# Projecting the first group of heads with whole 128-row products, over the pieces of x as they come, in a two-branch attention kernel

## The chip, the cores and the metric

The kernel runs on one core of a Trainium2 chip. The metric is the device time of one execution in microseconds. The time before is 974.14 us, the median of 3 runs (971.82 to 974.33).

## The reference

Two attention branches read the same x (2048 tokens, 640 features; 32 heads of 20) and are mixed by a gate per token:

```python
g = _sigmoid((x * gate_w).sum(-1, keepdims=True))
a = _A_ref(x, A_wq, A_wk, A_wv, A_wo, A_beta)
b = _B_ref(x, B_wqkv, B_wo)
return g * a + (1 - g) * b
```

Branch A cuts the tokens into 4 segments of 512. Within a segment it computes causal softmax attention, and beside it reads a memory that the earlier segments have left (a 20 x 20 matrix and a vector per head, with phi(t) = t + 1 for positive t, exp(t) otherwise); `beta` mixes the two per head. Branch B is causal attention over a sliding window of 256 tokens. Each branch has its own output projection.

So the work is: the projections q, k and v of both branches (each a product with 640 input features, in 5 pieces of 128), the scores, exponentials and weighted sums, the memory, and two output projections. The result is in float32.

## The kernel before, in words

**Precision.** Every large product is made of three. An operand is split into a high part (rounded to fp32r, ScalarE, line 541) and a low part (the remainder, GpSimd or VectorE, line 558), and a product is high x high, high x low and low x high (`PAIRS`), summed in PSUM.

**Turns and units.** The 64 heads of both branches make 4 groups of 16. A turn T is one group in one segment (16 turns; T = 0 and T = 1 are the first group of each branch in the first segment). A turn has 4 units u of 4 heads each. For a turn, five row tiles `("m", T, 0..4)` of 128 x 512 hold q and k of the 16 heads, and four value tiles `("v", T, 0..3)` hold the values of 128 tokens each.

**Projection by halves.** `plan_qk` takes two row tiles at a time. Each product has only 64 of the 128 rows of the contraction (`gemm2`, line 604): half of the array works for the one tile, the other half for the other, side by side. A weight tile (128 x 640) holds rows 0 to 63 for one tile and 64 to 127 for the other. After all 5 pieces of x the second weight tile comes, in which the halves are exchanged, so that both tiles get the missing half of their rows. Between the two phases a `join` (an empty instruction on ScalarE or VectorE) makes the second half wait for the first. Values are done in the same way, two token blocks at a time (`v_mm`, line 753). The last output projection of the kernel uses whole 128-row products instead (`gemm`, line 596).

**After a row tile.** ScalarE and VectorE copy it from PSUM as high and low parts (`m_high`, 625; `m_low`, 629; a ring of two buffers), for the memory also as phi (666 to 674), and SP stores it to DRAM (`qk_store`, 654 to 661: two stores for tiles 0, 1, 3, 4, six for tile 2). A unit reads its stack of q and k back from there (`stack_read`, line 827, 1 MB for branch A).

**A unit.** 16 products give the scores for the row maxima (`max_mm`, 857), reduced on VectorE (867, with the readout 867); the maxima go through DRAM into spare rows of the stack (887, 891); then come the scores again, transposed (`st_mm`, 914), the exponentials on ScalarE (921), causal masks on GpSimd (927, 930), the sum with the values (`av_mm`, 946), and for branch A the memory's read and update (977, 997).

**Order of the work.** Each instruction is put into a plan with a due time t, in which one unit is 1.0. `Plan.order` simulates the engines, the DMA queues and the 8 PSUM banks, and picks at each moment, among the instructions that can start soonest, the one with the smallest due time; the picked order is the order of each engine's queue, which then runs strictly in it. `SHIFT` and `NUDGE` move due times by kind of instruction and by stretch of the plan. All loads and stores are issued by SP, in this one order.

**The start.** The weights go through 2 staging buffers (`NWS`) into a ring of 3 split tiles (`NW`). In the order of due times the first weight tile comes, then the 5 pieces of x, then the second and third weight tile. A weight tile's load waits for a free staging buffer, that is, for the split of the tile two before it; the split waits for the last product of the tile three before it. SP also fills padding rows in DRAM (line 509), loads the values' weights (575, 805 KB), and loads pieces of x for the next segment (line 550) as soon as buffers are free. 26 small products warm PE up before the first real one (line 444).

Of the kernel before, what the change touches and what calls it, by code (L numbers as in the profile page):

```python
# [57 lines left out]
KINDS = dict(v_mm="v", max_mm="x", st_mm="s", tiled_mm="t", mem_add="a", split_h="h", split_l="l", m_high="e", m_low="e", v_out="e",  # L58
# [30 lines left out]
    d={3: -1.3, 5: 1.3, 8: 1.2, 11: -0.1, 12: 1.3, 24: -0.6, 37: -2.7},
    e={22: -1.3, 28: 0.1, 33: -0.2, 38: -1.1, 40: 1.1, 47: -0.2, 52: 4.6, 59: 1.3},  # L90
    h={18: -0.9, 25: -2.3, 37: 1, 38: -1.9, 73: 2.2},
    k={40: 0.9},
    l={62: 1.3},
    m={2: -0.28, 24: 0.5, 28: 0.2, 32: -0.11, 34: -0.015, 38: 0.77, 39: 0.514, 41: 0.5, 42: -0.05, 43: -0.318, 44: 1,
       48: -0.04, 52: -0.26, 56: -0.13, 59: 0.027, 61: -0.06, 66: -0.137},
    p={16: -0.4, 32: 1.8, 33: 1.2, 42: 0.56},
    q={4: -0.011, 18: 0.7, 42: 2.1, 47: 0.6, 52: 0.2, 53: -1.2},
    r={11: 0.2, 14: -0.04, 18: -0.7, 19: 1.5, 31: 0.6, 34: 0.06, 40: 2.9, 49: 0.03, 54: -2.2, 61: 2.1},
    s={6: 0.57, 13: 0.45, 17: 0.1, 21: 0.28, 24: -0.02, 25: -1.4, 28: 0.5, 30: 0.804, 37: 0.4, 40: -0.5, 41: -0.02,
       42: -0.5, 43: 0.075, 55: 0.2, 59: -4.3, 61: -2.4, 68: -1.2},  # L100
    t={41: 1.6, 60: 0.4},
    v={2: -0.17, 3: -0.174, 4: -1.506, 10: 0.03, 30: -0.007, 38: 0.023, 39: -0.123, 46: -0.1, 49: -0.002, 62: 0.3,
       63: 0.039, 64: -1.045, 67: -0.38},
    x={4: 0.05, 7: 0.44, 11: -0.53, 14: -0.17, 21: -0.15, 22: -0.01, 29: -0.17, 32: 0.5, 33: -0.4, 42: -0.13,
       46: 0.85, 49: -0.01, 50: 0.4, 52: -0.05, 56: 0.12, 68: -0.2, 69: 0.01, 70: 0.1, 71: 2.2},
    y={20: -0.004, 21: 0.17, 24: -0.53, 32: 0.04, 35: 0.044, 61: 0.23, 64: 0.106},
    z={4: 0.8, 6: 0.5, 11: 0.5},
    A={12: -0.34, 37: -3.8},
    I={0: -2.3},
    L={54: 1.411},  # L110
    M={6: -2.6, 7: -1, 13: -1, 20: -1.4, 22: -0.2, 29: -0.02, 52: 0.9, 56: 0.7, 65: 0.45},
    N={15: 1.6, 23: -0.3, 47: -0.2, 51: 0.1, 52: 0.6, 67: -0.2},
    O={6: 0.8, 7: 0.4, 10: 0.1, 13: 0.1, 34: -0.02, 51: 0.03, 68: 0.6, 69: 0.8},
    P={16: 2.4, 22: -0.4, 24: -2.9, 33: -1.3, 62: 1.3},
    Q={4: -0.238},
    S={11: 1.1, 22: 5.7, 63: 0.1},
# [1252 lines left out]
```

## Time and profile before

| | |
|---|---|
| median of 3 runs | 974.14 us (971.82 to 974.33) |
| profiled execution | 978.07 us |
| its span | 976.4 us |
| granted TensorE clock, mean | 0.996 |
| PE busy | 968.2 us (99%), 11295 products |
| VectorE, ScalarE, GpSimd busy | 760.6, 645.7, 632.5 us |
| DMA | 248.55 MB, mean 255 GB/s |

The span runs from the first to the last instruction; the rest of the time lies around it. PE busy counts time in which at least one product runs; two halves that run together count once, and a half that runs alone counts the same. The page's costliest groups are the half products of the projections: line 604 with 2400 products from x (456.8 us, mean 400 ns of one) and 1050 of the output projections (225.2 us), line 753 with 1920 (269.3 us). In the groups a form such as 64*128 64x512 is a stationary tile of 64 rows and 128 columns, and a moving operand of 64 rows and 512 columns.

### The profile page before, as it was taken

To read this page: it belongs to the slowest core of one execution; us is meant where nothing else is said; L and a number is where in the kernel's file an instruction comes from. 1 tells how busy PE (TensorE), PEld (TensorE's weight loads), DVE (VectorE), ACT (ScalarE), POOL (GpSimd) and SP (SyncE) were. 2 spreads that over 40 slices of the span, in tenths; PEclk is the share of its full clock that TensorE was granted. 3 is DMA by queue.
4 is the path that set the end of the run, shared out by engine and by line. 5 is a ranking of instruction groups with operands and counts; after the bars stand their busy time and mean duration, and the time that the engine had idled before them with its cause. 6 is when DMAs were issued, how large, how long until landed. Compare 5 with 4: busy or idle time off the path is not lost.

```text
span 976.4 us, 30303 instructions
## 1 busy us (share of the span) xinstructions
PE 968.2 (99%) x11295; PEld 813.3 (83%) x11295; DVE 760.6 (78%) x2629; ACT 645.7 (66%) x1432; POOL 632.5 (65%) x861
## 2 busy tenths in 40 slices
PE   9999999999999999999999999999999999999998
PEld 6998888888887888889888798888888888887786
DVE  3288889898989587889768878779777886789944
ACT  4436875886678676585857676676676666765672
POOL 4323766946775697666966578686696766965750
PEclk9998999999999999999999999999999999999999
DMA  9878899898998888879878788789877698485523
GB/s 312 283 247 270 283 296 292 233 323 245 315 271 281 279 237 265 255 245 333 263 218 269 253 297 254 230 243 310 296 252 243 198 304 273 159 263 195 186 88 125
DMA packets 155379, 248.55 MB, mean 255 GB/s; under 512 B 51104, under 2 KB 64672, under 8 KB 155232
## 3 DMA queue, kind: packets, MB, share of 16 engines
q1 hardware_dynamic: 155232, 246.62, 79.2%
q8 instruction: 89, 1.46, 0.6%
q14 instruction: 58, 0.48, 0.1%
HBM read 150.88 MB, written 95.68 MB: 253 GB/s over the span
## 4 chain that ended last, share of the span: by engine, by line
PE 90%; DMA 4%; DVE 3%; issue 1%; ACT 0%; SPq 0%; POOL 0%; DVEq 0%; ACTq 0%
PE bank L604 42%; PE bank L946 15%; PE bank L753 14%; PE bank L857 8%; PE bank L914 8%; DVE bank L867 2%; PE bank L596 1%; DMA wst<-wqk 1%; PE bank L977 1%; DMA qks<-dmx 1%; PE bank L997 1%; DMA wvs<-wv 1%; DMA qks<-dqk 1%; DMA dqk<-ml 0%; DVE ys L1101 0%
## 5 line engine op out<-in xcount | busy, mean ns | idle before, releaser
L921 ACT ACTIVATE P<-bank 128x512 f32<-128x512 f32 (+2 forms) x768 | 378.6, 559 | 123.0 <-PE bank L914 69.3
L604 PE MATMUL bank<-xhl,w 64*128 64x512 f32 x2400 | 456.8, 400 | 0.6 <-ACT w L541 0.4
L604 PEld LDWEIGHTS bank<-xhl,w 64*128 64x128 f32 x2400 | 326.1, 186 | 15.1 <-issue 1.6
L857 PE MATMUL bank<-qks 64*128 64x384 f32 (+7 forms) x1024 | 304.3, 333 | 1.1 <-DMA qks<-dqk 0.9
L867 DVE CUSTOM_DVE_ANT_0 bank<-bank,mask_b 128x384 f32<-128x384 f32 (+2 forms) x512 | 259.9, 555 | 26.6 <-PE bank L857 18.2
L753 PE MATMUL bank<-wv,xhl 64*128 64x320 f32 (+1 forms) x1920 | 269.3, 312 | 0.5 <-POOL wv L558 0.4
L867 DVE CUSTOM_DVE_ANT_0 bank<-bank,mask_a 128x384 f32<-128x384 f32 (+3 forms) x512 | 240.2, 511 | 33.0 <-PE bank L857 22.1
L914 PE MATMUL bank<-qks 64*128 64x384 f32 (+3 forms) x1216 | 256.0, 301 | 0.3
L753 PEld LDWEIGHTS bank<-wv,xhl 64*128 64x128 f32 x1920 | 230.2, 185 | 3.7 <-issue 0.8
L604 PE MATMUL bank<-ohl,w 64*128 64x512 f32 x1050 | 225.2, 398 | 0.9 <-issue 0.6
L927 POOL TENSOR_SCALAR_AFFINE_SELECT P<-P 128x512 f32<-128x512 f32 x256 | 161.5, 639 | 82.4 <-ACT P L921 70.8
L558 POOL TENSOR_TENSOR w<-wst,w 128x640 fp32r<-128x640 f32 x110 | 171.8, 1566 | 59.8 <-ACT w L541 59.1
L914 PEld LDWEIGHTS bank<-qks 64*128 64x128 f32 x1216 | 192.8, 185 | 16.9 <-issue 4.1
L857 PEld LDWEIGHTS bank<-qks 64*128 64x128 f32 (+1 forms) x1024 | 177.4, 185 | 17.0 <-issue 6.7
L946 PE MATMUL bank<-P,vau 128*32 128x384 f32 (+3 forms) x2432 | 159.8, 407 | 0.2 <-DVE mx L867 0.2
L604 PEld LDWEIGHTS bank<-ohl,w 64*128 64x128 f32 x1050 | 151.6, 185 | 7.2 <-issue 2.8
L867 DVE DVE_READ_ACCUMULATOR2_ANT mx<- 128x1 f32 x1024 | 144.1, 141 | 0.0
L946 PEld LDWEIGHTS bank<-P,vau 128*32 128x32 f32 x2432 | 69.3, 109 | 77.8 <-issue 60.6
L541 ACT ACTIVATE w<-wst 128x640 fp32r<-128x640 f32 x121 | 90.0, 747 | 39.6 <-PE bank L604 21.1
L1021 DVE STREAM_TRANSPOSE ot<-bank 128x512 f32<-128x512 f32 x64 | 45.7, 714 | 67.3 <-PE bank L946 58.9
L558 POOL TENSOR_TENSOR wv<-wvs,wv 128x322 fp32r<-128x322 f32 x80 | 65.1, 832 | 17.8 <-ACT wv L541 17.4
L930 POOL TENSOR_SCALAR_AFFINE_SELECT P<-P 128x512 f32<-128x512 f32 x112 | 70.7, 641 | 8.6 <-ACT P L921 7.2
(73 smaller groups left out, 761.1 us busy)
## 6 DMA issues: line engine op xcount, KB each, us to landing
qks<-dqk SPq DMA_DIRECT2D x32, 1024.0 KB
wst<-wqk SPq DMA_DIRECT2D x80, 320.0 KB
qks<-dkb SPq DMA_DIRECT2D x24, 768.0 KB
dqk<-ml SPq DMA_DIRECT2D x32, 512.0 KB
qks<-dqb SPq DMA_DIRECT2D x32, 512.0 KB
o_dram<-ot SPq DMA_DIRECT2D x64, 256.0 KB
wst<-wo SPq DMA_DIRECT2D x41, 320.0 KB
wvs<-wv SPq DMA_DIRECT2D x16, 805.0 KB
```

The source lines that it names most:

```text
L541: nc.scalar.activation(dst, src, AF.Copy)
L558: EN[e].tensor_tensor(out=t[:, 1], in0=B.pop(src), in1=f(t[:, 0]), op=ALU.subtract)
L604: z = nc.tensor.matmul(B[key], B[wkey][64 * r:64 * r + 64, a, 128 * c:128 * c + 128], B[xkey, c][64 * r:64 * r + 64, b], start=start, stop ...
L753: z = nc.tensor.matmul(B["v", T, b][:, :n], B[("x", s), c][64 * r:64 * r + 64, a, 128 * b:128 * b + 128], B["wv", T, c][64 * r:64 * r + 64 ...
L857: nc.tensor.matmul(psum(("mx", u, p, b, r))[:, :n], fr(q), keys(u, K, r, p, c0, n), start=True, stop=True)
L867: nc.vector.tensor_tensor_reduce(out=x, in0=x, in1=mk, scale=1.0, scalar=BIG, op0=ALU.add, op1=ALU.max, accum_out=B["M", u][:, j:j + 1])
L914: nc.tensor.matmul(B[k][:, c:c + 128 * n], keys(u, K, r, p, WIN + 128 * kb, 128), fr(q[64 * r:64 * r + K, L * p + 128 * q0:L * p + 128 * ( ...
L921: nc.scalar.activation(B["P", u, b][:, 2 * r + p, c0:c1], B["st", u, b, p, r][:, c0:c1], AF.Exp, scale=SCALE)
L927: nc.gpsimd.affine_select(out=v, in_=v, pattern=[[0, 4], [1, 128]], compare_op=ALU.is_ge, fill=0.0, base=0, channel_multiplier=-1)
L930: nc.gpsimd.affine_select(out=v, in_=v, pattern=[[0, 4], [-1, 128]], compare_op=ALU.is_gt, fill=0.0, base=0, channel_multiplier=1)
L946: nc.tensor.matmul(o[32 * j:32 * j + 32, 128 * q0:128 * (q0 + n)], v[:, VA * h:VA * h + 32], t[:, j, c:c + 128 * n], start=(b == 0 and i = ...
L1021: nc.vector.transpose(t, B["o", u])
```

## The change

The first turn (T = 0) is projected with whole 128-row products.

- Row tiles 0, 1 and 2 run over the pieces of x together: for a piece c the products of all three tiles, then piece c + 1; then tile 3 over all pieces, then tile 4, then row tile 0 of turn 1. `FIRST` is this order. A product is `gemm1`.
- The weights for it come as a new input `w0`, six tiles of five 128 x 128 blocks, in the order in which `FIRST` uses them. The first tile holds (tile 0, c 0), (1, 0), (2, 0), (0, 1), (1, 1).
- The four value tiles of turn 0 are whole products too (`v_whole`, 322 columns), one token block after the other. Both have no `join`, and may take up to 7 PSUM banks where the halves take up to 5.
- In the order of loads the first three weight tiles and the pieces of x alternate: w0, x0, w1, x1, w2, x2, x3, x4.
- `NUDGE` is replaced by another table, so the order of all work is planned anew. `SHIFT` and the plan's other numbers stay. Turn 1's other tiles and all later turns are projected by halves as before.

```diff
+FIRST = [(m, c) for c in range(NC) for m in range(3)] + [(m, c) for m in (3, 4) for c in range(NC)]
-KINDS = dict(v_mm="v", max_mm="x", ...
+KINDS = dict(v_mm="v", v_whole="v", gemm1="m", max_mm="x", ...
 NUDGE = dict(
-    c={18: -0.9, 38: 1.1, 55: 0.5, 60: -0.6, 66: -0.2, 68: 0.5, 69: 1.4},
+    c={10: 2.5, 15: 1, 24: 0.03},
...
-    W={0: 4.8, 6: 1.7, 12: 0.2},
-    Y={52: 1.1, 55: 0.14})
+    W={0: 6.4, 29: -2.7, 37: -2.2})
...
+    def gemm1(key, wkey, xkey, c, i, col):
+        if c == i == 0:
+            psum(key)
+        a, b = PAIRS[i]
+        nc.tensor.matmul(B[key], B[wkey][:, a, col:col + 128], B[xkey, c][:, b],
+                         start=c == i == 0, stop=c == NC - 1 and i == 2)
+
+    def plan_chunk(t, dt, key, wkey, xkey, c, col):
+        for i in range(3):
+            add(t + i * dt / 3, PE, 0.229, gemm1, key, wkey, xkey, c, i, col, bank=("pj", NPP + 2, key) if c == i == 0 else (),
+                mod=[key] if c or i else [], get=[wkey, (xkey, c)] if i else [("first", wkey), ("first", (xkey, c))],
+                pace=P0, cols=512, mode=("wide", 0.2))
+
+    def plan_first(t, dt):
+        for n, (m, c) in enumerate(FIRST):
+            wkey = ("w", "first", n // NC)
+            if n % NC == 0:
+                tiles.append((t + n * dt, t + (n + NC) * dt, wkey, w0[n // NC]))
+            plan_chunk(t + n * dt, dt, ("m", 0, m), wkey, ("x", 0), c, 128 * (n % NC))
+            if c == NC - 1:
+                plan_m(t + (n + 1) * dt - 0.01, 0, m)
+        tc = t + NC * (NC - 1) * dt
+        t, wkey = tc + NC * dt, ("w", ("m", 1, 0))
+        tiles.append((t, t + NC * dt, wkey, w0[NC]))
+        for c in range(NC):
+            plan_chunk(t + c * dt, dt, ("m", 1, 0), wkey, ("x", 0), c, 128 * c)
+        plan_m(t + NC * dt - 0.01, 1, 0)
...
+        if T == 0:
+            return plan_first(t, dt) if m == 0 else None
         plan_pair(t, dt, z, [("x", s)] * 2, [wqk[T % 4 // 2, i + ph] for ph in range(2)])
...
+    def v_whole(T, b, c, i):
+        if c == i == 0:
+            psum(("v", T, b))
+        g, s = head(T)
+        a, bb = PAIRS[i]
+        nc.tensor.matmul(B["v", T, b][:, :VW], B[("x", s), c][:, a, 128 * b:128 * b + 128], B["wv", T, c][:, bb, :VW],
+                         start=c == i == 0, stop=c == NC - 1 and i == 2)
+
     def plan_v(t, dt, T, b):
         g, s = head(T)
+        for j in range(2 * (T == 0)):
+            k, tj = ("v", T, b + j), t + j * NC * dt
+            for n in range(3 * NC):
+                c, i = divmod(n, 3)
+                add(tj + n * dt / 3, PE, 0.146, v_whole, T, b + j, c, i, bank=("pj", NPP + 2, k) if n == 0 else (),
+                    mod=[k] if n else [], get=[("wv", T, c), (("x", s), c)] if i else [("first", ("wv", T, c)), ("first", (("x", s), c))],
+                    pace=P0, cols=322, mode=("wide", 0.12))
+            plan_vout(tj + NC * dt - 0.01, T, b + j)
+        if T == 0:
+            return
...
-                plan_split(-20 + 0.02 * c, -20.01 + 0.02 * c, "xhl", xpool, NX, "ys", NC, L, (("x", 0), c),
+                plan_split(-20 + 0.2 * c, -20.01 + 0.2 * c, "xhl", xpool, NX, "ys", NC, L, (("x", 0), c),
...
-        at.append(max(tiles[i - NW][1], at[-1] + 0.004) if i >= NW else -18 + 0.1 * i)
-        plan_split(at[i], at[i - 1] + 0.002 if i else -21, "w", wpool, NW, "wst", NWS, D, wkey, src)
+        at.append(max(tiles[i - NW][1], at[-1] + 0.004) if i >= NW else -19.995 + 0.2 * i)
+        plan_split(at[i], at[i - 1] + 0.002 if i >= NW else -20.02 + 0.2 * i, "w", wpool, NW, "wst", NWS, D, wkey, src)
...
+    def turn_first(w):
+        b = [w[128 * c:128 * c + 128, 128 * m:128 * m + 128] for m, c in FIRST]
+        return np.stack([np.concatenate(b[i:i + NC], 1) for i in range(0, NC * NC, NC)])
...
+                beta=n(n(A_beta).reshape(8, 4).T), w0=n(np.concatenate([turn_first(qk[0]), wt[2][:1]])))
```

More of the change, by code (lines that the diff above doesn't have):

```diff
@@ L57 @@
 EPS = 1e-6
-KINDS = dict(v_mm="v", max_mm="x", st_mm="s", tiled_mm="t", mem_add="a", split_h="h", split_l="l", m_high="e", m_low="e", v_out="e",
+FIRST = [(m, c) for c in range(NC) for m in range(3)] + [(m, c) for m in (3, 4) for c in range(NC)]
+KINDS = dict(v_mm="v", v_whole="v", gemm1="m", max_mm="x", st_mm="s", tiled_mm="t", mem_add="a", split_h="h", split_l="l", m_high="e", m_low="e", v_out="e",
              y_out="e", phi_neg="p", phi_exp="p", phi_sum="p", max_red="r", st_exp="c", select="k", load="d", wv_load="d",
@@ L87 @@
 NUDGE = dict(
-    c={18: -0.9, 38: 1.1, 55: 0.5, 60: -0.6, 66: -0.2, 68: 0.5, 69: 1.4},
[L89 to L116, printed above, removed]
-    W={0: 4.8, 6: 1.7, 12: 0.2},
-    Y={52: 1.1, 55: 0.14})
+    c={10: 2.5, 15: 1, 24: 0.03},
+    d={2: -1.7, 3: -2.4, 8: -0.4, 14: 0.4, 15: 1.1, 16: 3.2, 22: -0.8, 30: 0.8, 43: -0.4, 61: 0.6},
+    e={21: -1.1, 31: 2.6, 33: 0.4, 38: -1, 42: 0.3, 49: -0.1, 60: -1, 64: 0.1},
+    h={10: -0.6, 12: 1.7, 19: 0.13, 30: 2, 40: -0.8, 59: 0.24, 64: 0.3, 66: -0.1, 73: 1.9},
@@ new lines @@
+    k={45: 1.8, 58: 1},
+    l={31: -0.9},
+    m={1: 1.67, 2: 0.925, 8: -3.5, 17: -0.076, 26: 0.096, 29: -0.017, 34: -0.053, 38: 0.554, 42: 0.1, 43: -0.38,
+       44: 0.103, 47: 0.3, 48: 0.03, 56: 0.09, 59: -0.025, 61: -0.01, 62: 0.31, 63: 0.015},
+    p={32: 1.5, 43: 0.7, 60: 1},
+    q={7: -0.9, 8: -3.2, 9: -0.9, 16: -0.6, 28: 1, 34: 2.9, 37: 2.9, 43: 0.2},
+    r={20: 0.03, 22: 0.01, 24: -2.2, 26: 0.01, 35: 1.2, 47: -0.17, 50: -1.8, 51: 1, 56: 1.2, 71: -1.6},
+    s={15: 0.1, 20: -0.22, 22: 0.1, 30: 0.324, 34: 1.8, 41: -0.3, 43: -0.04, 45: 0.2, 51: 0.23, 56: 0.18, 57: 0.3,
+       59: -0.1, 63: -0.01, 65: -0.4, 68: 0.2, 70: -0.6, 72: -0.1, 73: 2.855},
@@ new lines @@
+    t={31: 0.1, 42: 1.2, 45: 3.1, 50: -0.3, 51: 0.8},
+    v={1: 0.488, 2: -0.14, 17: 0.02, 18: -0.14, 20: -0.06, 26: 0.25, 27: -0.03, 30: 0.01, 31: -0.8, 35: -0.086,
+       38: -0.06, 39: -0.559, 45: 0.31, 47: 0.01, 48: -0.005, 53: -0.033, 62: -0.045, 63: -0.1, 67: -0.66},
+    x={6: -0.67, 17: -1.6, 27: 0.05, 31: 0.4, 33: 0.06, 39: -0.22, 40: -0.16, 43: -0.04, 45: 0.36, 49: 0.045,
+       52: -0.07, 59: 0.028, 61: -0.06, 68: 0.1},
+    y={20: -0.02, 21: 0.34, 28: 0.33, 29: 0.44, 42: 0.5, 45: 0.13, 51: -0.945, 56: -0.14, 63: 0.028, 66: -0.15,
+       72: -2.01, 73: 0.12},
@@ L121, in f @@
+    z={7: -1.3, 37: -0.1},
+    A={7: -0.7, 11: -1.9, 27: -0.15},
+    M={4: -1.8, 21: -1.8, 47: -0.01, 56: 0.2},
+    N={7: -0.5, 16: 0.1, 24: -0.6, 51: 0.1, 61: -0.02},
+    O={10: 1.7, 12: 0.3, 14: 1.5, 16: -0.4, 45: 0.1, 59: -0.11, 68: 2.7, 70: 0.15, 71: -0.3, 72: 1.4},
+    P={23: -0.7, 34: 1.8, 42: -0.35, 51: 0.4},
+    Q={5: 5.1, 9: -1.6, 23: -0.44, 41: -2.2, 46: 1},
+    R={42: 0.2},
+    S={19: 0.9},
+    W={0: 6.4, 29: -2.7, 37: -2.2})
 def f(ap):
@@ L413, in gated_mix_kernel @@
 @with_exitstack
-def gated_mix_kernel(ctx: ExitStack, tc: tile.TileContext, xt, wqk, wv, wo, beta, out):
+def gated_mix_kernel(ctx: ExitStack, tc: tile.TileContext, xt, wqk, wv, wo, beta, w0, out):
     nc = tc.nc
@@ L420, in gated_mix_kernel, with attention @@
     o_dram = [dram.tile([H, 32, S], F32, name=f"o_dram{i}") for i in range(2)]
-    attention(ctx, tc, const, dram, xt, wqk, wv, wo, beta, o_dram, out)
-def attention(ctx, tc, const, dram, xt, wqk, wv, wo, beta, o_dram, out):
+    attention(ctx, tc, const, dram, xt, wqk, wv, wo, beta, w0, o_dram, out)
+def attention(ctx, tc, const, dram, xt, wqk, wv, wo, beta, w0, o_dram, out):
     nc = tc.nc
```

1 line of the change is left out of this document (removed).

## The prediction

> **What bounds the kernel now.** First the page: its header, and the shares of the chain of waits.
>
> ```profile
> span 976.4 us, 30303 instructions
> ...
> PE 90%; DMA 4%; DVE 3%; issue 1%; ACT 0%; SPq 0%; POOL 0%; DVEq 0%; ACTq 0%
> ```
>
> The profiled execution took 978.07 us, 1.7 more than its span; the median of the runs is 974.14. The chain runs through PE for 90% of the span, so a microsecond that PE wastes anywhere is a microsecond of the end. "Busy" doesn't show the waste: two half-array products run at once, and one alone is busy too. So I price the products and count them. The prices come from runs without gaps: two from the timeline (start, length, group), the third from the chain.
>
> ```profile
> 10.67 7.18 PE L604 MATMUL bank<-xhl,w 64*128 64x512 f32 x60 [0.18 <-ACTq L619]
> 24.49 4.06 PE L753 MATMUL bank<-wv,xhl 64*128 64x322 f32 x49
> ```
>
> ```profile
> 955.31 14.54 PE bank L596 x63
> ```
>
> L596 is the whole 128-row product that the end of the kernel already uses: 14.54 / 63 = 0.231 us for 512 columns. A half of 64 rows costs (7.18 - 0.39 for the last one's own length) / 59 = 0.115, so a pair costs 0.231 too. A half of a value product (322 columns) costs (4.06 - 0.31) / 48 = 0.078, the pair 0.156. The prices times the counts below say how full PE really was. The columns are window, length, busy time and count, clock, DMA share, GB/s; first L604, then L753, L857 and L914.
>
> ```profile
> 6.46:17.90 11.44, 11.21 (x90) 1.00 1.00 336
> 17.90:21.30 3.40, 1.04 (x4) 1.00 1.05 405
> 36.70:43.80 7.10, 5.82 (x29) 1.00 0.82 309
> 54.80:74.20 19.40, 12.29 (x49) 1.00 0.74 209
> 74.20:82.20 8.00, 7.73 (x24) 0.57 1.01 344
> 150.00:350.00 200.00, 128.04 (x669) 1.00 0.90 280
> ```
>
> ```profile
> 17.90:21.30 3.40, 2.65 (x21) 1.00 1.05 405
> 36.70:43.80 7.10, 2.52 (x11) 1.00 0.82 309
> 54.80:74.20 19.40, 13.70 (x107) 1.00 0.74 209
> 150.00:350.00 200.00, 68.55 (x476) 1.00 0.90 280
> ```
>
> ```profile
> 54.80:74.20 19.40, 9.28 (x34) 1.00 0.74 209
> 74.20:82.20 8.00, 4.24 (x12) 0.57 1.01 344
> 150.00:350.00 200.00, 69.76 (x244) 1.00 0.90 280
> ```
>
> ```profile
> 74.20:82.20 8.00, 2.16 (x5) 0.57 1.01 344
> 150.00:350.00 200.00, 61.61 (x268) 1.00 0.90 280
> ```
>
> For L857 and L914, of 128 to 512 columns, I take 0.08 a half, an estimate, some two thirds of the 0.115 of 512 columns. Work against time:
> 6.46 to 17.9: 90 x 0.115 = 10.4 of 11.4, lost 1.0.
> 17.9 to 21.3: 0.5 + 1.6 of 3.4, lost 1.3.
> 36.7 to 43.8: 3.3 + 0.9 of 7.1, lost 2.9.
> 54.8 to 74.2: 5.6 + 8.3 + 2.7 of 19.4, lost 2.8.
> 74.2 to 82.2, at 0.57 of the clock: 2.8 + 1.4 of 8.0, lost 3.8.
> Together 11.8 us. In 150 to 350 it is 77 + 37 + 41 and the output products of L946 (34.94 busy), 190 of 200, with the small memory products not counted: later PE is full. So the change can win in the first 82 us and hardly elsewhere. The order planned anew reaches the rest too; I set that at 0, and since at most 10 in 200 are open, and a worse order can open as much, I allow 3 us either way for what a reshuffle leaves.
>
> ```profile
> 150.00:350.00 200.00, 34.94 (x504) 1.00 0.90 280
> ```
>
> Why PE lost it: timeline rows of the weights' loads (L550), their first split on ScalarE (L541), and what stood between.
>
> ```profile
> 6.46 4.03 PE L604 MATMUL bank<-xhl,w 64*128 64x512 f32 x30
> ...
> 10.66 0.46 SPq L575 DMA_DIRECT2D wvs<-wv  x1
> ...
> 11.21 1.78 SPq L550 DMA_DIRECT2D wst<-wqk  x2
> ...
> 14.49 1.09 ACT L625 ACTIVATE ml<-bank 128x512 fp32r<-128x512 f32 x2 [2.71 <-PE bank L604]
> ...
> 18.94 0.74 ACT L541 ACTIVATE w<-wst 128x640 fp32r<-128x640 f32 x1 [0.34 <-DMA wst<-wqk]
> ...
> 27.51 1.57 POOL L558 TENSOR_TENSOR w<-wst,w 128x640 fp32r<-128x640 f32 x1 [2.27 <-ACT w L541]
> ...
> 27.95 4.63 SPq L661 DMA_DIRECT2D dqk<-ml  x6
> ...
> 34.82 1.15 SPq L550 DMA_DIRECT2D wst<-wqk  x2
> ...
> 36.65 1.09 ACT L625 ACTIVATE ml<-bank 128x512 fp32r<-128x512 f32 x2 [5.93 <-PE bank L604]
> ```
>
> ```profile
> 43.07 1.35 ACT L541 ACTIVATE w<-wst 128x640 fp32r<-128x640 f32 x2
> 45.89 0.74 SPq L827 DMA_DIRECT2D qks<-dqk  x1
> ...
> 47.65 0.66 SPq L827 DMA_DIRECT2D qks<-dqk  x1
> ...
> 54.83 0.45 PE L857 MATMUL bank<-qks 64*128 64x128 f32 x2
> ```
>
> The fourth weight tile is issued at 11.21, behind the values' weights of 10.66 on queues at share 1.00, and is split only at 18.94: the loss of 17.9. The eighth could be issued once POOL has done the sixth's low part (27.51 + 1.57 = 29.1); SP sits in the six stores of the third row tile (27.95 to 32.6) and the stores behind them, issues at 34.82, and the tile is split at 43.07, 8.25 us later: the loss of 36.7. By then the values, which PE could have done meanwhile, are half gone (the x49 at 24.49). The third loss is a transfer, in the chain (start, length):
>
> ```profile
> 68.02 6.02 DMA qks<-dqk
> ```
>
> Loads three and four of the stacks follow the first two (45.89, 47.65) 20 us late; PE stands at a product on one of them until 74, and then runs at about half clock to 82.
>
> **The change, part by part.** *Whole products for the first group.* Removed: 150 + 30 halves of L604 (five row tiles of group 0, one of group 1) and 120 of L753, with their joins. Added: 75 + 15 whole products of 512 columns and 60 of 322. The first: 180 x 0.115 = 20.8 before, 90 x 0.231 = 20.8 after: 0. For the second no whole product of 322 columns is in the trace. From below it is 0.231 x 322 / 512 = 0.145, from above the 0.231 of 512 columns; between them lies its weight load of 0.188, from the row just below. The pair's 0.156 is the nearest row, with the same columns and the same 128 stationary columns in each half; I take it: 60 x 0.156 = 9.4, as before. Ends: -0.7 and +4.5; +1.9 if the load sets the pace.
>
> ```profile
> L596 PEld LDWEIGHTS bank<-ohl,w 128*128 128x128 f32 x75 | 14.0, 188 | 3.3 <-ACT ys L1098 0.4
> ```
>
> That row also shows 188 ns of loading inside a pace of 231 while the product streams, so loads of the whole array hide. The Trainium skill ("TensorE: Matmul & The Clock Gate", Part 3, "The mechanism") says against this change that weight loads overlap with running products only where the row group differs; by that rule every whole product would pay its load, the sum would be some 28 us worse, and the trace, with 231, doesn't bear it out for 512 columns.
>
> The joins go from ScalarE's and VectorE's queues; the one that shows cost 0.18 (the x60 row), inside the 1.0.
>
> *Switches.* Whole products and halves now meet between 24 and 60 us, where whole values serve as filler among halves. The trace has no such switch. The nearest is one product of 512 columns between two blocks of 32-column tiles, in the chain:
>
> ```profile
> 86.52 0.43 PE bank L857
> ```
>
> 0.43 - 0.23 = 0.2 for two switches, 0.1 each. From below a switch is free. I count ten: 1.0, ends 0 and 2. The Trainium skill ("TensorEngine Tiling (Array Packing)", Key Properties) says that a change of tiling mode drains the engine; the trace agrees with 0.1.
>
> *Order of loads.* The second and third weight tiles move ahead on SP into the pieces of x: w0, x0, w1, x1, and so on (w2 still has to wait for w0's staging buffer). The second piece of x lands 0.33 MB at 336 GB/s = 1.0 us later. That is covered: with w0 and x0 PE has three row tiles, 9 x 0.231 = 2.1 us, to 8.5, where it had 0.7 us per piece. Without the cover it is 1.0, once. PE's start at 6.46 hangs on w0 and x0, which stay first: 0. Of the first loss of 1.0 I give back 0.7 (ends 0 and 1.0).
>
> The fourth tile needs w1's staging free. w1 now lands ahead of x1, some 4 us sooner than in the old place behind all of x, so the fourth is split near 15 (18.94 - 4). PE needs it after 15 blocks of 0.69, at 6.46 + 10.4 = 16.9. Of 1.3 I give back 1.3 (0 to 1.3).
>
> *Values later.* Row tiles 0 to 2 end together near 16.9, tile 3 at 20.4, tile 4 at 23.8, the first of group 1 at 27.3; before, tiles 0 and 1 ended at 14.5 and tile 4 only at 36.65. So 9.4 us of values are left for the time when the seventh and eighth weight tiles are late. Of the 2.9 I give back 2.2; ends 0 and 2.9.
>
> *Three tiles at once.* Their stores are 2 + 2 + 6 issues, where the six alone hold SP 4.63 us, and the ring behind L625 has two buffers; weights five and six queue behind them. Cost 0 while values cover, taken at 0.5, up to 5 (the slower rival).
>
> *Attention's start.* Keys and queries of group 0 are complete 36.65 - 23.8 = 12.8 us sooner, so stacks can be loaded sooner, and more projection is left as filler when the first maxima run. Whether loads three and four still come late is the new order's doing. Of 2.8 + 3.8 I take half, 3.3; ends 0 and 6.6.
>
> Sum: -0.7 - 1.3 - 2.2 - 3.3 + 1.0 + 0.5 = -6.0. Against the profiled execution 978.07 - 6.0 = 972.1; the median lies 3.9 below that execution, so 974.1 - 6.0 = 968.1.
>
> **Rivals.** *A, the sum: 968.1*, within 964.5 to 971.5.
>
> *B, hidden anyway: 973.5.* The queues are at 1.00 to 1.05 until 21 us and the bytes are the same. If stacks and weights come no sooner, the idle time of 17.9 and 36.7 only moves to the wait near 68: the 4.2 won by then is given back but for 0.6. For it: those DMA shares. Against it: the shares of 0.74 and 0.82 after 36.7, so the queues have room, and SP's order, not bytes, made the lateness.
>
> *C, the stall goes as well: 964.8.* All 6.6 after 54.8 is won, 3.3 more than in A. For it: one late pair of loads causes it. Against: before it the queues already carry the stores of group 1, and they remain.
>
> *D, slower: the burst of stores starves PE: 982.* The ten stores take 4 x 0.4 + 4.63 = 6.2 us of SP. If they stand ahead of weights six and seven, and those take the 8.25 us to land that the eighth took, the tiles come 14.5 us late; values cover 9.4. PE idles 5.1 and afterwards loses the clock, another 3.8 as at 74.2; with 1.0 for switches that is 9.9, against 0.7 and 1.3 won before: 974.1 + 7.9. It decides from the point where more stores than some four go ahead of those loads. For it: exactly this happened at 27.95. Against: w5's staging frees before the stores begin.
>
> *E, whole loads don't hide: 150 x 0.188 = 28 us, less 6: 996.* The 0.231 of L596 speaks against; only the 322 columns are unseen. It is what the rule quoted above from the Trainium skill ("TensorE: Matmul & The Clock Gate", Part 3) would make of the change.
>
> **How the numbers follow.** A 0.46, B 0.21, C 0.14, D 0.16, E 0.03. The predicted time is A's, 968.1. From 961.8 (C less the 3 us of reshuffling) up to 978 the range leaves out E, most of D and the tail of C: some 2 in 10. Within 0.3%, 2.9 us, nothing can be told from no change. Faster: C, A but for its upper tenth, a little of B: 0.57. Same: the rest of A and most of B, 0.25. Slower: D, E: 0.18.
>
> **What would show it.** Right: a run of whole products from 6.46 with 0.23 us each and no gap to 27; the fourth weight tile split before 17; L625 of the fifth row tile near 24; the first maximum before 48 where it was at 54.8; no window at half clock near 75. Wrong: whole values spaced over 0.19; the stores of L661 ahead of weight loads with PE idle behind; the clock below 0.9 in any window up to 90; or a 150 to 350 in which the counts fall, which would say that the new order and not the start made the time.

## The result, and the profile after

The kernel after takes 967.36 us (median of 12 runs, 965.85 to 974.30), the kernel before 972.54 in the same series (12 runs): a ratio of 0.9942, 95% interval 0.9923 to 0.9962. That is 5.2 to 5.6 us faster, where the prediction said 968.1 and 6.0 faster. One run of `halves_paired` below took 4495.85 us; its median and its ratio are those of the other nine. The page of the kernel after, its header and the shares of its chain:

```profile
span 972.6 us, 30007 instructions
...
PE 89%; DMA 5%; DVE 2%; issue 1%; ACT 1%; SPq 1%; POOL 0%; DVEq 0%; POOLq 0%; ACTq 0%
```

This profiled execution took 974.30 us, 7 above its own median, so the two first profiles can't simply be subtracted. One reason shows in a window of this execution (window, length, busy time and count of PE, PEld, DVE, ACT and POOL, then clock, DMA share, GB/s):

```profile
370.00:390.00 20.00, 18.71 (x219) 13.19 (x219) 11.49 (x35) 9.17 (x19) 7.22 (x10) 0.91 0.82 261
```

The clock falls there, far from the change. A second profile of each kernel was therefore taken, in which the mean clock is 1.000 for both: spans 972.0 (before) and 966.1 (after), 5.9 apart. Where the text says "second profile", it is this pair.

The start of the kernel after, PE's timeline (start, length, group, idle time before it and what ended it). L702 is the whole row product `gemm1`, L826 the whole value product `v_whole`, L906 the first product for the maxima (L857 before):

```profile
5.12 2.58 PE L702 MATMUL bank<-xhl,w 128*128 128x512 f32 x9
8.35 11.00 PE L702 MATMUL bank<-xhl,w 128*128 128x512 f32 x47 [0.64 <-ACT xhl L541]
19.85 0.57 PE L826 MATMUL bank<-wv,xhl 128*128 128x322 f32 x2 [0.51 <-ACT wv L541]
...
24.04 2.56 PE L826 MATMUL bank<-wv,xhl 128*128 128x322 f32 x16
...
53.38 0.33 PE L906 MATMUL bank<-qks 60*128 60x128 f32 x2 [0.26 <-DMA qks<-dqk]
```

The prices hold. 47 whole row products run at (11.00 - 0.39) / 46 = 0.231 us, and 16 whole value products at (2.56 - 0.31) / 15 = 0.150, where 0.156 was taken. The clean run is not quite free of gaps: 0.64 at the second piece of x, 0.51 at the values' weights; in the second profile 0.69 and 1.12. Of the loads, only the second weight tile moved ahead in the end: SP's queue has w0, x0, w1, then the other four pieces of x from 2.18 on, and w2 at 6.11. ScalarE's timeline in the first profile, for the second piece of x, the fourth weight tile and the copies of the third and fifth row tile:

```profile
7.66 2.54 ACT L541 ACTIVATE xhl<-ys 128x512 fp32r<-128x512 f32 x4 [0.86 <-DMA ys<-xt]
...
13.78 0.74 ACT L541 ACTIVATE w<-wst 128x640 fp32r<-128x640 f32 x1 [1.99 <-DMA wst<-w]
...
28.24 0.60 ACT L625 ACTIVATE ml<-bank 128x512 fp32r<-128x512 f32 x1 [0.74 <-DMA dqk<-ml]
...
35.26 0.59 ACT L625 ACTIVATE ml<-bank 128x512 fp32r<-128x512 f32 x1
```

The losses of 36.7 to 43.8 and after 54.8 are all but gone. The windows of the second profile of before, all engines:

```profile
36.70:43.80 7.10, 6.70 (x40) 5.57 (x38) 1.92 (x3) 3.01 (x6) 0.00 (x0) 1.00 0.83 312
54.80:74.20 19.40, 19.40 (x198) 18.45 (x197) 18.80 (x77) 5.01 (x11) 3.57 (x4) 1.00 0.81 237
74.20:82.20 8.00, 7.97 (x97) 6.93 (x95) 7.87 (x35) 5.79 (x15) 2.26 (x5) 1.00 0.98 327
```

and of the second profile of after:

```profile
36.70:43.80 7.10, 6.91 (x55) 5.33 (x55) 2.06 (x6) 4.31 (x14) 0.72 (x1) 1.00 1.00 314
54.80:74.20 19.40, 19.38 (x209) 18.53 (x208) 19.09 (x81) 5.66 (x12) 5.49 (x6) 1.00 0.89 301
74.20:82.20 8.00, 8.00 (x79) 7.29 (x77) 7.41 (x32) 6.44 (x16) 1.55 (x3) 1.00 0.86 244
750.00:950.00 200.00, 199.99 (x2222) 162.22 (x2219) 156.93 (x517) 132.28 (x280) 133.43 (x186) 1.00 0.64 209
```

PE's busy time is nearly the same in both, but in 36.7 to 43.8 it holds 55 products instead of 40. The window 74.2 to 82.2 stands at clock 1.00 before as well: the 0.57 of the first profile is not there in every execution.

The prediction's own measure (length less count times price, with 0.150 for a whole value product) gives this for the second profiles and, in brackets, the first ones, in us lost by PE:

| window | before | after |
|---|---|---|
| 6.46 to 17.9 | 1.3 (1.1) | 0.6 (0.4) |
| 17.9 to 21.3 | 1.3 (1.3) | 1.0 (0.3) |
| 21.3 to 36.7 | 0.3 (0.3) | -0.4 (-0.1) |
| 36.7 to 43.8 | 2.9 (2.9) | 0.5 (0.6) |
| 43.8 to 54.8 | -0.1 (0.3) | 0.5 (0.6) |
| 54.8 to 74.2 | 1.9 (2.7) | 0.5 (0.5) |
| 74.2 to 82.2 | 1.3 (3.9) | 0.0 (0.2) |
| 82.2 to 950 | 20.8 (21.3) | 20.0 (25.6) |

By the second profiles, 8.9 - 2.7 = 6.2 us are won by 82.2 and 0.8 in all the rest. Their sum, 7.0, is 1.1 more than the spans' difference of 5.9. What lies ahead of 6.46 and after 950, missing records and the rounded price of the smaller products are in that 1.1; I don't split it.

### The profile page after: what moved, and what is told of

It reads as the page before. It is cut to its first block, busy times and chain, and to the rows that moved or that the text cites. A ratio compares the mean times of both kernels' runs of the same rounds, so it can differ in the third digit from the quotient of the medians.

```text
span 972.6 us, 30007 instructions
## 1 busy us (share of the span) xinstructions
PE 961.1 (99%) x11145; PEld 800.3 (82%) x11145; DVE 759.7 (78%) x2626; ACT 649.4 (67%) x1433; POOL 634.2 (65%) x863
## 4 chain that ended last, share of the span: by engine, by line
PE 89%; DMA 5%; DVE 2%; issue 1%; ACT 1%; SPq 1%; POOL 0%; DVEq 0%; POOLq 0%; ACTq 0%
PE bank L604 39%; PE bank L995 15%; PE bank L784 14%; PE bank L963 9%; PE bank L906 9%; DMA qks<-dqk 2%; PE bank L596 1%; PE bank L1026 1%; DVE bank L916 1%; DMA dmx<-mt 1%; DMA wvs<-wv 1%; PE bank L1046 1%; PE bank L826 1%; DMA ys<-xt 1%; PE bank L702 0%
## 5 line engine op out<-in xcount | busy, mean ns | idle before, releaser
L604 PE MATMUL bank<-xhl,w 64*128 64x512 f32 x2220 | 421.3, 397 | 0.3 <-ACTq L619 0.2
L906 PE MATMUL bank<-qks 64*128 64x384 f32 (+7 forms) x1024 | 306.5, 331 | 2.4 <-DVE ys L1150 1.3
L604 PEld LDWEIGHTS bank<-xhl,w 64*128 64x128 f32 x2220 | 298.3, 185 | 8.4 <-issue 1.7
L916 DVE CUSTOM_DVE_ANT_0 bank<-bank,mask_b 128x384 f32<-128x384 f32 (+2 forms) x512 | 258.9, 556 | 20.8 <-PE bank L906 14.5
L916 DVE CUSTOM_DVE_ANT_0 bank<-bank,mask_a 128x128 f32<-128x128 f32 (+3 forms) x512 | 239.0, 513 | 37.5 <-PE bank L906 25.1
L963 PE MATMUL bank<-qks 64*128 64x384 f32 (+3 forms) x1216 | 253.3, 301 | 3.0 <-ACT P L970 1.4
L784 PE MATMUL bank<-wv,xhl 64*128 64x320 f32 (+1 forms) x1800 | 252.4, 313 | 0.0
L784 PEld LDWEIGHTS bank<-wv,xhl 64*128 64x128 f32 x1800 | 213.1, 185 | 3.3 <-issue 2.1
L963 PEld LDWEIGHTS bank<-qks 64*128 64x128 f32 x1216 | 189.9, 184 | 24.2 <-issue 5.5
L906 PEld LDWEIGHTS bank<-qks 64*128 64x128 f32 (+1 forms) x1024 | 178.3, 184 | 19.1 <-issue 4.6
```

What stands on the lines that cost most here:

```text
L604: z = nc.tensor.matmul(B[key], B[wkey][64 * r:64 * r + 64, a, 128 * c:128 * c + 128], B[xkey, c][64 * r:64 * r + 64, b], start=start, stop ...
L784: z = nc.tensor.matmul(B["v", T, b][:, :n], B[("x", s), c][64 * r:64 * r + 64, a, 128 * b:128 * b + 128], B["wv", T, c][64 * r:64 * r + 64 ...
L906: nc.tensor.matmul(psum(("mx", u, p, b, r))[:, :n], fr(q), keys(u, K, r, p, c0, n), start=True, stop=True)
L916: nc.vector.tensor_tensor_reduce(out=x, in0=x, in1=mk, scale=1.0, scalar=BIG, op0=ALU.add, op1=ALU.max, accum_out=B["M", u][:, j:j + 1])
L963: nc.tensor.matmul(B[k][:, c:c + 128 * n], keys(u, K, r, p, WIN + 128 * kb, 128), fr(q[64 * r:64 * r + K, L * p + 128 * q0:L * p + 128 * ( ...
```

## The experiments

All moves of a single load or product were made after the planner: the planned order is taken as a list, one entry is moved, and the rest is left as it is. So the work is the same and only the order of the queues differs.

### Both kernels once more

No edit; timed again, with a fresh profile each.

> The kernel before, unchanged, for a second profile of it. If the half clock between 74 and 82 us belongs to the kernel, the profile shows a window there with a granted clock near 0.57 again, and the mean clock of the timed runs is near 0.996 as in the first profile. If it belongs to that one execution, the clock is 1.00 there, the profiled time is near the median of 972.5 instead of 5 us above it, and the 3.8 us that the prediction put down to that window were never there to be won in a usual run. Ratio to before: 1.000 by both.

> The changed kernel, unchanged, for a second profile and a second ratio. Expected 0.994 of before by every theory. If the first profile's 7 us above the median belong to that execution, this profile lies within 2 us of the median, and its PE counts between 150 and 950 us show where the first one lost time.

Before against itself: 0.9998 (0.9982 to 1.0014). After: 967.36 us, ratio 0.9940 (0.9922 to 0.9957). These profiles gave the table above. The loss of before after 54.8 is 1.9 + 1.3 = 3.2 us and not 6.6; the other 3.4 came with the low clock of the first execution.

A lower clock somewhere is not rare in the kernel before: of its 92 timed runs here with a clock on record, 33 have a mean clock of 0.998 or less (0.996 in the first profile), of the 18 of the kernel after one. Where it fell in those runs is not recorded. It is not what makes the change faster: the runs at 0.999 and above alone have medians of 972.5 before and 967.2 after.

### Is the start on the path at all?

```diff
-for i in range(WARM):
+for i in range(WARM + 44):
```

> The changed kernel, the same order on every engine, with 44 more of the small warm-up products ahead of the first real one: PE starts its real work about 44 x 0.107 = 4.7 us later (estimate from the 26 in 4.55 us of the changed kernel, of which the first part is at half clock). Theory: PE bounds the kernel from the first product on, a microsecond lost at the start is one at the end; 967.4 + 4.0 to 4.7, ratio to before 0.998 to 0.999, and the gain of the change is gone for the most part. Rival: other limits (loads, VectorE's maxima) hold the end and the start has slack; then less than half of it arrives, below 969.5, ratio 0.996 or less.

PE's first real products in the kernel after and, at the end, its first long run of values; first its second profile, then the experiment:

```profile
5.40 2.35 PE L702 MATMUL bank<-xhl,w 128*128 128x512 f32 x9
8.43 11.00 PE L702 MATMUL bank<-xhl,w 128*128 128x512 f32 x47 [0.69 <-ACT xhl L541]
20.55 0.57 PE L826 MATMUL bank<-wv,xhl 128*128 128x322 f32 x2 [1.12 <-ACT wv L541]
...
21.65 2.11 PE L826 MATMUL bank<-wv,xhl 128*128 128x322 f32 x13
```

```profile
10.26 12.97 PE L702 MATMUL bank<-xhl,w 128*128 128x512 f32 x56
...
24.05 2.11 PE L826 MATMUL bank<-wv,xhl 128*128 128x322 f32 x13
```

The first product comes 4.86 us later, and the waits of 0.69 for the second piece of x and of 1.12 for the values' weights are gone with it: the thirteen values start at 24.05 instead of 21.65, 2.40 late. The time is 970.82, ratio 0.9967 (0.9950 to 0.9984): 2.4 us later by the ratios (0.9967 - 0.9942), 3.5 by the medians. The interval of each ratio is about 1.7 us either way, so the size is rough; it fits a start that is on the path, where what PE still lags by after the first loads arrives at the end.

### The order of the first loads

In the kernel after, SP's order set back: pieces 1 to 4 of x right behind piece 0, ahead of the second weight tile. ScalarE's order stays as planned.

```diff
+for c in range(1, 5):
+    # load of piece c of x goes right behind the load of piece c - 1
+    move("load", (("x", 0), c), behind="load", where=(("x", 0), c - 1))
```

> The changed kernel with one thing moved in SP's order: pieces 1 to 4 of x are loaded ahead of the second weight tile, as before the change. In the profile of the change PE stood 0.64 us at 7.7 for piece 1, and its weights came early. Theory: the order of these loads only moves about 1 us between two places: piece 1 comes sooner (0.6 won), the second and with it the fourth weight tile later (up to 1.3 lost at 17 to 21); ratio to before 0.994 to 0.996. Rival: the alternation of weights and pieces is the part that makes the whole products pay; then PE stands for the second weight tile near 10 and for the fourth near 17, 3 us or more are lost, ratio 0.997 to 1.000.

970.7 us, ratio 0.9973 (0.9957 to 0.9990): 3.0 us of the gain are gone. ScalarE and PE of this kernel:

```profile
9.24 0.74 ACT L553 ACTIVATE w<-wst 128x640 fp32r<-128x640 f32 x1 [4.10 <-DMA wst<-w]
```

```profile
10.55 11.25 PE L714 MATMUL bank<-xhl,w 128*128 128x512 f32 x47 [2.17 <-ACT xhl L553]
...
22.62 2.11 PE L838 MATMUL bank<-wv,xhl 128*128 128x322 f32 x13
```

Pieces of x are issued earlier, but ScalarE's queue has the second weight tile's split ahead of the second piece's, and stands 4.10 us at it. PE waits 2.17 instead of 0.69. Load order and split order belong together; this run tests a mismatch of the two, not the old order as such. And it doesn't price even that: PE no longer waits for the values' weights, so its thirteen values start at 22.62 against 21.65, 0.97 late, and 0.67 of this is the start itself (6.07 instead of 5.40), which differs between executions of one kernel. The spans of the two profiles, 968.9 and 966.1, are 2.8 apart. So 1.8 of it is lost after 22 us, where the order is the same, and I can't place it.

Then the other way, to take the waits at 8 and 19 us out. The second piece of x is loaded and split right behind the first, and the values' weights are loaded right behind the fourth weight tile; the second kernel also has 10 warm-up products fewer.

```diff
+# load and both splits of piece 1 of x right behind those of piece 0
+move("load", x1, behind="load", where=x0)
+move("split_h", x1, behind="split_h", where=x0)
+move("split_l", x1, behind="split_l", where=x0)
+# the values' weights right behind the fourth weight tile
+move("wv_load", 0, behind="load", where=("w", "first", 3))
...
-for i in range(WARM):          # second kernel only
+for i in range(WARM - 10):
```

> The changed kernel with two things moved and nothing else: the second piece of x is loaded and split ahead of the second weight tile (on SP, ScalarE and VectorE), and the load of the values' weights goes ahead of three fillings of padding rows, right behind the load of the fourth weight tile. In the profiles of the change PE stood 0.64 and 0.69 us for that piece at 7.7, and lost 0.3 and 1.0 between 17.9 and 21.3, where the values' weights had just landed. Theory (PE bounds from the first product on, and whole products only wait for what lands late): both waits go, 1.0 to 1.7 us of PE, 0.7 to 1.7 of the time: 966, ratio 0.992 to 0.993 of before. Rival: what is moved ahead makes another load late by as much; 967 to 968, ratio 0.994.

> The run before this one with 10 fewer of the small warm-up products (16 instead of 26, the order kept). The warm-up ended at 6.46 in the first profile of before and at 5.1 to 5.4 in those of the change, and the first pieces are split from 5.1 on. Theory: PE starts at 5.1 in every execution, 0 to 0.5 us sooner than the run before; time the same to 0.5 lower. Rival: with less warm-up the clock falls to half or comes up later, PE's first products run at half clock for up to a window of 3.4 us, and the time is 1 to 2 us above the run before.

967.64 (ratio 0.9943, 0.9924 to 0.9962) and 968.07 (0.9948, 0.9932 to 0.9964): neither differs from the kernel after. PE of the first:

```profile
8.43 8.47 PE L719 MATMUL bank<-xhl,w 128*128 128x512 f32 x36 [0.26 <-ACT w L558]
17.64 2.33 PE L719 MATMUL bank<-xhl,w 128*128 128x512 f32 x9 [0.74 <-POOL w L575]
```

and of the second:

```profile
5.20 15.27 PE L719 MATMUL bank<-xhl,w 128*128 128x512 f32 x56 [0.80 <-ACT xhl L558]
```

The 0.69 and 1.12 left and 0.26 and 0.74 came, now for weights: the DMA share is 1.01 to 1.04 from 7 to 11 us in the first of these kernels, and moving one load ahead makes another late. In the second kernel 56 products without a gap take 15.27 us where (55 x 0.231 + 0.39) = 13.1 would do: with 16 warm-up products the first real ones ran slower. So neither order wins anything that these runs can show; a gain below the 1.6 to 1.9 us of their intervals would not be seen.

### What made the loss of 36.7 to 43.8

The prediction blamed the eighth weight tile, which waits behind stores on SP. In the kernel before it is loaded ahead of them, and the ninth with it:

```diff
+move("load", ("w", 1, ("m", 1, 1)), behind="split_l", where=("w", 1, ("m", 0, 4)))
+move("load", ("w", 0, ("m", 1, 3)), behind="split_l", where=("w", 0, ("m", 1, 1)))
```

> The kernel before with only the loads of the eighth and ninth weight tile moved ahead on SP, without the moved stacks. The prediction put the loss of 2.9 us at 36.7 to 43.8 down to the late eighth tile: then it falls below 1.5 us and the ratio is 0.997 to 0.999. By the theory that halves without a partner make that loss it stays at 2.5 to 2.9 us, and the ratio is 0.999 to 1.001.

973.64 us, ratio 1.0006 (0.9990 to 1.0023): nothing. SP of this kernel, then ScalarE, then PE:

```profile
28.18 0.33 SPq L562 DMA_DIRECT2D wst<-wqk  x1
```

```profile
42.16 1.35 ACT L553 ACTIVATE w<-wst 128x640 fp32r<-128x640 f32 x2
```

```profile
35.92 2.60 PE L616 MATMUL bank<-xhl,w 64*128 64x512 f32 x12
...
38.35 2.47 PE L616 MATMUL bank<-xhl,w 64*128 64x512 f32 x11
```

A weight load now goes out at 28.18, ahead of the stores, and its tile can be there long before 42; still it is split only at 42.16, and the window loses 2.5. The reason is in PE's rows, and it stood in the profile before just so. Twelve halves take 2.60 us: (2.60 - 0.39) / 11 = 0.20 each, not 0.115. They run alone. PE's queue has thirteen halves of row tile (1, 2) first and then those of (1, 1), so that none of them has its partner next to it. ScalarE's `join`, its phi and the split of the weights then queue behind the end of these lone halves; second profile of before, ScalarE:

```profile
42.51 0.63 ACT L670 ACTIVATE phi<-phi 128x512 f32<-128x512 f32 x1 [3.93 <-PE bank L604]
```

So the lone halves were put side by side, in the kernel before and nothing else changed:

```diff
+# all but the first and the last half of ("m", 1, 2) with the weights ("w", 0, ("m", 1, 1)) go
+# right behind the half of ("m", 1, 1) with the same piece c and the same pair i (13 halves)
+for half in halves[1:-1]:
+    move("gemm2", half, behind="gemm2", where=(("m", 1, 1), half.c, half.i))
```

> The kernel before with one thing moved in PE's order: the thirteen halves of row tile 2 of turn 1 that run alone from 36.8, on one half of the array, are moved behind, each next to a half of row tile 1 of turn 1, which in before runs alone from 39.2 on the other half. Theory from the runs so far (the loss at 36.7 to 43.8 is halves that run without a partner, 0.2 us each in place of 0.115, because the partner's PSUM bank comes free only near 39): PE now stands from about 36.8 to 39, then runs pairs at 0.23, and is done no sooner; the loss in that window stays at 2.4 to 2.9 us, ratio 0.999 to 1.001. Rival: only the written order kept the halves apart; pairs run from 36.9, the loss in the window falls by 1.4 us or more, ratio 0.998 to 0.999.

970.8 us, ratio 0.9970 (0.9956 to 0.9984): 2.9 us faster, 1.6 to 4.3. The stretch from the last run of pairs to the twenty values, in the second profile of before:

```profile
32.99 3.83 PE L604 MATMUL bank<-xhl,w 64*128 64x512 f32 x29
...
44.16 1.65 PE L753 MATMUL bank<-wv,xhl 64*128 64x322 f32 x20
```

and PE of this kernel, then the window:

```profile
32.43 3.72 PE L622 MATMUL bank<-xhl,w 64*128 64x512 f32 x30
...
36.17 3.15 PE L622 MATMUL bank<-xhl,w 64*128 64x512 f32 x25
...
41.09 1.65 PE L771 MATMUL bank<-wv,xhl 64*128 64x322 f32 x20
```

```profile
36.70:43.80 7.10, 7.10 (x67) 6.59 (x65) 2.07 (x3) 4.38 (x8) 3.02 (x2) 1.00 0.97 353
```

25 halves in 3.15 us, (3.15 - 0.39) / 24 = 0.115: pairs again, 67 products in a window that held 40. The stretch takes 41.09 - 32.43 = 8.66 us where it took 11.17 (and 11.17 again with the moved weights), 2.5 less, and the loss in the window falls from 2.9 to 0.5. I had expected nothing of this run, taking the second tile's PSUM bank to come free too late; it doesn't. So about half of what the change wins can be had in the kernel before by moving 13 products on one queue.

### What made the loss after 54.8

The prediction laid it to loads three and four of the stacks, issued 20 us late. In the kernel before they go out right behind the second; once alone, once with the weights' loads of the last section:

```diff
+move("stack_read", (2, 0), behind="stack_read", where=(1, 0))
+move("stack_read", (3, 0), behind="stack_read", where=(2, 0))
```

> The kernel before with one thing moved in SP's order and nothing else: the loads of the third and fourth stack (68.02 us in the profile of before) go right behind the load of the second (47.65). Theory of the prediction, third loss: their lateness, by SP's order, makes PE stand near 68 to 74; then PE fills there, and the time falls by 2.8 us (without the half clock) up to 6.6 (with it): ratio 0.993 to 0.997. Rival, the transfers only move: the 2 MB delay the loads and stores that now come behind them, PE stands elsewhere, ratio 0.999 to 1.002.

> The kernel before with the stack loads moved as in the run before this one, and the loads of the eighth and ninth weight tile (34.82 us in the profile of before) moved ahead on SP, right behind the split that frees their staging buffer, that is, in front of and between the six stores of the third row tile. All products stay halves. If the losses at 36.7 and 68 come from SP's order alone, both go: 2.9 us more than the run with the stacks alone, 5.7 to 9.5 in all, ratio 0.990 to 0.994, as good as the change itself without a single whole product. If the values left over as filler are what the change brings, the gap at 36.7 stays (the values are used up by then) or moves to the stores behind, and the ratio is that of the run with the stacks alone.

976.66 (ratio 1.0031, 1.0013 to 1.0050) and 976.16 (1.0031, 1.0011 to 1.0051): both slower, by 3 us. SP of the first, then its chain, then the waits of ScalarE and PE from 50 to 70, then its windows:

```profile
46.99 3.36 SPq L839 DMA_DIRECT2D qks<-dqk  x3
```

```profile
52.47 13.36 DMA wst<-wqk
```

```profile
ACT w L553 <- DMA wst<-wqk: 10.7, 2, 10.4
...
PE bank L869 <- ACT vau L553: 3.9, 1, 3.9
```

```profile
64.00:67.00 3.00, 0.00 (x0) 0.00 (x0) 0.00 (x0) 1.06 (x3) 0.25 (x1) 0.70 0.37 126
67.00:70.00 3.00, 2.95 (x20) 2.95 (x22) 1.98 (x8) 1.02 (x3) 1.48 (x2) 0.50 0.94 244
```

The three stack reads (3 MB) stand ahead of the next weight tile, which takes 13.36 us to land. ScalarE's in-order queue stands at that tile's split for 10.4 us, the values' copies behind it free no bank, PE stands 3.9 us for one of them (no product from 64 to 67), and then the clock is down to 0.50. Late stacks were not the loss by themselves: bringing them ahead of weights is worse than leaving them late. With the weights' loads moved as well it is no better. In the kernel after, three of the four stack reads go out at 44.44 and 46.93, early without this harm, and there the next weight tile goes out only 14 us later; SP of the kernel after, first profile:

```profile
44.44 0.37 SPq L876 DMA_DIRECT2D qks<-dqk  x1
...
46.93 2.65 SPq L876 DMA_DIRECT2D qks<-dqk  x2
...
60.97 0.35 SPq L550 DMA_DIRECT2D wst<-wqk  x1
```

That this makes the difference is read from the two orders; no run shows it by itself.

What made the 3.2 us of before after 54.8 stays open for the most part. Neither earlier weights (2.0 lost in 54.8 to 74.2, as before) nor earlier stacks took it away, and pairing the thirteen halves leaves it too (2.0 and 0.7). PE is not idle there: in the second profile of before it is busy for 19.40 of 19.40 us, and in the first it stands once, 0.9 us, for a stack (PE's waits, 54 to 82):

```profile
PE bank L857 <- DMA qks<-dqk: 0.9, 1, 0.9
```

A part is lone halves again (second profile of before):

```profile
70.92 1.76 PE L604 MATMUL bank<-xhl,w 64*128 64x512 f32 x8
...
74.10 1.00 PE L604 MATMUL bank<-xhl,w 64*128 64x512 f32 x4
```

(1.76 - 0.39) / 7 = 0.196 and (1.00 - 0.39) / 3 = 0.203 us each; the eight all belong to row tile (2, 0) and have none of (2, 1) next to them. Against 0.115 these twelve cost some 1.0 us more, an estimate. Pairing them was not tried.

### What the new table is worth in the rest

The kernel after with the old `NUDGE` from step 35 on (437 us), and the kernel before with the new one from step 14 on (175 us):

```diff
-NUDGE = dict(...)                                   # one table
+NUDGE = {group: {step: old[group][step] if step >= 35 else new[group][step]}}
...
+NUDGE = {group: {step: new[group][step] if step >= 14 else old[group][step]}}
```

> The changed kernel with the new table of shifts up to 437 us of the plan, and the table of before from there on; the first 437 us of the order stay as they are. Theory: the gain is made at the start, ratio to before 0.993 to 0.997, near the 0.994 of the change. Rival: the order planned anew brings a good part of it in the later stretches, ratio 0.997 or more.

> The kernel before with its own table of shifts up to 175 us of the plan and the new table from there on; all products halves, and the start as before. Theory: without the new start nothing is won; ratio 1.000, or up to 1.006, since the new table was not made for this start. Rival, the new order of the rest is what gains: ratio 0.994 to 0.997.

1028.62 us (ratio 1.0566, 1.0539 to 1.0594) and 1022.47 (1.0500, 1.0473 to 1.0526): 61 us over the kernel after, 49 over the kernel before. A window of the first, all engines:

```profile
750.00:950.00 200.00, 197.05 (x1972) 156.09 (x1969) 141.53 (x490) 114.08 (x241) 113.87 (x155) 0.97 0.63 202
```

PE is busy for 197 of these 200 us and does 1972 products where the kernel after does 2222. Again the count tells what the busy time hides: by the prices PE loses 30.6 us there against 9.4. The same entries are good behind their own start and bad behind the other, so in both trials a part of a table could not be moved from one order to another, and these two runs don't price the replanning. What it brings in the rest is, net, the 0.8 us of the table in the first section.

Not tried: row tiles whole with the values by halves, the reverse, the load order alone, and a third buffer for the row tiles' copies. So no run takes the change apart into its pieces.

## Why the prediction was right, and where it was not

The total was right: -6.0 forecast, -5.2 to -5.6 measured. Term by term, by the second profiles:

**What bounds.** Right. PE is still 89% of the chain, counts times prices follow the time in both kernels, and a start that left PE 2.4 us late by 24 us cost 2.4 to 3.5 at the end.

**Whole products, 0; whole values at 0.156.** Right in kind. At 0.150 a value product the 60 of them cost 9.0 us instead of 9.4. The rule cited in the prediction from the Trainium skill ("TensorE: Matmul & The Clock Gate", Part 3, "The mechanism"), by which weight loads overlap with running products only where the row group differs, is contradicted by both rows: 0.231 with 512 columns and 0.150 with 322, the latter below the 0.189 of a single load of its own (weight loads of the kernel after, first profile). Rival E is out.

```profile
L826 PEld LDWEIGHTS bank<-wv,xhl 128*128 128x128 f32 x60 | 9.7, 189 | 1.6 <-ACT wv L541 0.9 <-issue 0.2
```

**Switches, +1.0.** Overrated in number, underrated each. Ten were counted; whole rows and whole values mix without a switch, and three remain, near 37 (PE of the kernel after, first profile):

```profile
36.33 0.46 PE L826 MATMUL bank<-wv,xhl 128*128 128x322 f32 x2
36.72 0.50 PE L604 MATMUL bank<-xhl,w 64*128 64x512 f32 x2
37.14 0.41 PE L826 MATMUL bank<-wv,xhl 128*128 128x322 f32 x1
37.49 3.46 PE L604 MATMUL bank<-xhl,w 64*128 64x512 f32 x28
```

From 36.33 to 37.49 are 1.16 us for three whole values and a pair, 3 x 0.150 + 0.231 = 0.68: 0.48 for three switches, 0.16 each. It is most of the 0.6 lost in that window.

**Loss of 6.46 to 17.9, -0.7.** Measured 1.3 to 0.6, -0.7. The second piece of x was split 1.4 us later (7.66 against 6.25 in the first profiles), not 1.0, so the cover was 0.6 short. The third weight tile did not move ahead.

**Loss of 17.9 to 21.3, -1.3.** The fourth weight tile is split at 13.78 and not at 18.94, as said. But PE then waits for the values' weights instead, and -0.3 (second profiles) to -1.0 (first) came of it.

**Loss of 36.7 to 43.8, -2.2.** Measured 2.9 to 0.5, -2.4: the size was right, and the cause wrong. The step that failed is "the eighth could be issued once POOL has done the sixth's low part ... the loss of 36.7". Loading a weight tile at 28.18 changed nothing; pairing the lone halves brought 2.9 us. The 8.25 us from issue to split were not a transfer either: ScalarE stood behind the lone halves until 42.51, and with the pairs it splits the same tile at 39.98, its load not moved. The prediction had the row in hand, the 5.82 of busy time for 29 products, that is 0.20 each, and read it as idle time around a late tile. Whole products have no partner to lose, and by 36.7 the kernel after has done the first tile of turn 1 whole; its halves run in pairs.

**Loss after 54.8, -3.3 of 6.6.** Measured 3.2 to 0.5, -2.7. Two errors cancel: half of the 6.6 came with one execution's clock, and of the other half nearly all was won, not half. The step that failed is "PE stands at a product on one of them until 74": the 6.02 is the length of a transfer, and PE stood 0.9 us in that execution and not at all in the second. The cause named, late stack loads by SP's order, fell: moved ahead they cost 3 us. But for some 1.0 us of lone halves the real one is open.

**Three at once, +0.5.** The burst is there: the third tile's products are done near 16.7 (8.35 + 36 x 0.231), and its copy waits for the ring until 28.24, released by a store. Values filled PE meanwhile, and the term is 0. Rival D did not come.

**Attention's start.** Wrong: keys 12.8 us sooner, first maximum before 48. The fifth row tile's copy is at 35.26 (36.65 before) and the first maximum at 53.38 (54.83). PE put values in between, in the order planned. It cost nothing, as PE was full; but no gain of the change comes from an earlier attention.

**The replanned rest, 0 ± 3.** The 0 was near: 0.8 won. But it is the sum of larger moves. By the same measure (the products of the weighted sums and of the memory at their busy time) PE loses 5.6 us in 150 to 350 against 3.4 before, and 1.6 in 350 to 750 against 5.5 (second profiles). So a sign that the prediction named for being wrong, counts that fall in 150 to 350, did come, and the new order made up for it later. The 0.8 itself can't be told from nothing: `whole_late`, `whole_old_loads`, `whole_x1_values` and `whole_better` have the same order of the rest and lose 1.4 to 2.4 us more from 82.2 to 950 than the second profile of after. The ± 3 fits a table made for the order; with half of a table made for another it was 49 to 61 us, which the prediction did not see.

**Half clock.** "No half clock near 75" is met, but proves little, since the second profile of before has none there either.

So the sum came out right partly by luck: the two largest terms had about the right size, and the causes given for them fell. Of the gain, the runs show the cause of about half, the lone halves of 36.7 to 43.8.

## What to carry to other kernels

Where two half-array products are to share the array, price them from the count and not from the busy time, and look in PE's queue whether the partners stand next to each other: 13 products moved were worth 2.9 us, half of this change. Moving a load ahead on a full queue makes another one late, and an in-order engine that stands at that one's split carries the wait to everything behind it. A profile's slowest stretch should be seen in a second execution before it is explained, and due times tuned for one order are not a part that can be kept when the order changes.

## What the runs showed of the hardware that I had not expected

- A product of 64 rows alone takes 0.20 us for 512 columns, and two side by side 0.231: alone it costs nearly as much as the pair.
- The same 26 warm-up products took between 4.46 and 5.70 us from execution to execution, so the first real product starts anywhere from 5.1 to 6.5 us.
- The clock fell to 0.57 for 8 us in one execution of the kernel before and not in the next, and in one of the kernel after to 0.91 over 20 us at a quite different place (370). The spans of these two executions are 4.4 and 6.5 us above those of the second profiles.
- A weight tile that was there within 7.5 us in the kernel before (issued at 53.20, split at 60.72 after a wait for PE) took 13.36 to land with three stack reads, 3 MB, issued ahead of it.
